# Building a product's weight operands during an earlier stage, and ordering gates and operand splits by hand, in an attention and feed-forward kernel

## Chip, cores and metric

One core of a Trainium2 chip runs the whole program in one launch. The metric is the device time of one execution in microseconds (us). PE is TensorE (matmuls), DVE VectorE, ACT ScalarE, POOL GpSimd, and SP the engine that issues all DMAs here.

## What is computed

Packed attention, then two feed-forward layers over 4608 tokens:

```python
def sm_attn(qq, kk, vv):                    # softmax(scale * q k^T) v
    ...
p_packed = sm_attn(p, k, v)                 # 8 batches x 8 heads, 32 packed rows of 64
out = sm_attn(q, p_packed, p_packed)        # 576 rows of each batch
x = out.transpose(0, 2, 1, 3).reshape(4608, 512)
x = ((x @ w_a) * (x @ w_b)) @ w_out         # 512 -> 1536 -> 512
h = x @ w_in                                # 512 -> 2048
g = h * np.clip(h + 3.0, 0.0, 6.0) / 6.0
return g @ w_out2                           # 2048 -> 512
```

All is float32; the weights reach the kernel as 64-bit words and are rounded on the chip.

## The kernel before

**Matmuls.** A float32 operand is split into `hi`, its value rounded to the matmul's type (a cast on ACT), and `lo`, the rest (a subtraction on DVE or POOL). `mm3` (L59) makes a product from three matmuls: hi by hi, hi by lo, lo by hi (L60 to L62).

**First stage: four groups of two batches.** A group has 12 steps, one for each 128 of the first layer's 1536 inner columns, 48 steps in all. A step has four `ab_unit`s (12 matmuls of 288 columns into `ab`; ACT copies one half to `a`, L440, DVE multiplies it by the other, L442, and ACT and POOL split the result `g`, L448 and L449), one `pw_unit` (32 small matmuls into `pw`, L411) and about five `y_unit`s (nine matmuls into `y`; ACT or DVE adds them up, L467 and L469). Between these lie ten slots for background work, listed in `todo` and `parts`: group one rounds the first layer's weights, groups two and three round the 32 pieces of the second layer's `w_in` and `w_out2`, and groups one to three carry the next group's attention. The order on every engine is that of the program's text; each engine works its own list in order.

**Rounding.** `f64_load` and `f64_round` (L64 to L99) take one piece of 128 x 512 words from DRAM through two ACT, three DVE and one POOL operation. `piece_units` cuts this in five units; the rounded piece, `p2f`, is stored to DRAM.

**Group four** runs `w_prep` as its background: 16 jobs, eight for `w_out2`, then eight for `w_in`. A job loads two rounded pieces into `raw_w`, makes four sums on POOL (L519 to L523), splits the seven blocks of a Strassen-like product into one tile `w` (four casts on ACT, L534, and four subtractions on DVE, L535) and stores it to `wo2d` or `w2d` in DRAM. The tile `w` has a single buffer. The last units of `bg` load y, the first layer's output, and split it for the second stage.

**Second stage.** Six blocks of 768 tokens, eight products in a block. A product takes a 256-column slice of `w_in` through seven partial products of six matmuls of 384 columns, in the order 1, 6, 2, 7, 5, 4, 3. ACT copies the first (`s`, L925), DVE adds (`u`, L776, and `b`, L948, L955, L962). `gate` (L781) is a ReLU on ACT (`r`, L784) and a minimum and multiplication on DVE (L785); two POOL operations after a product's last gate make `t2` (L967 to L969). Four products are a quad, and its *out product* (with `w_out2`) is cut into 28 units of six matmuls into `o`. While a quad's products run, one unit of the quad before follows each partial product: `o_slot` first issues the splits of the units up to two ahead (`o_split`: `oh` on ACT, L805; `ol` on DVE, L806; some with a POOL subtraction), but of no unit of a quad that is not finished, then the unit's matmuls. After the last product 28 units remain. In a block's last product `swap(k)` also splits the next block's y operands (`yh`, `yl`, L585 and L586).

```python
        def o_slot(ready):
            n = n_unit[0]
            if n >= 28 * ready:
                return
            while n_unit[1] < min(n + 1 + LEAD, 28 * ready):    # LEAD = 2
                o_split(*units[n_unit[1]])
                n_unit[1] += 1
            o_unit(*units[n])
            n_unit[0] += 1
```

Of the kernel before, what the change touches and what calls it, by code (L numbers as in the profile page):

```python
# [22 lines left out]
P = 128  # L23
# [23 lines left out]
def tile_kernel(ctx: ExitStack, tc: tile.TileContext, qT, kT, vn, pT, wab, wo1, win, wo2, out):  # L47
# [16 lines left out]
    def f64_load(pool_, src, name, bufs=AHEAD):  # L64

        raw = pool_.tile([P, CP], mybir.dt.uint64, tag="f64", name=f"f64{name}", bufs=bufs)
        sp.dma_start(raw, src)
        return raw

    def f64_round(pool_, raw, dst, name, bufs=2):  # L70
# [9 lines left out]
        def a0():  # L80
            z["sq"] = pool_.tile([P, CP], F32, tag="cv_sq", name=f"cv_sq{name}", bufs=bufs)
            act.activation(z["sq"], w.bitcast(F32), AF.Square)
            act.activation(dst.bitcast(I32), low, AF.Copy, scale=2.0 ** -13)
            z["a"] = pool_.tile([P, CP], U32, tag="cv_a", name=f"cv_a{name}", bufs=bufs)
            dve.tensor_scalar(z["a"], w, 3, 0x3FFFFFFF, op0=ALU.logical_shift_left, op1=ALU.bitwise_and)
# [18 lines left out]
    p2f = dram.tile([NM2, 2, P, CP], F32, name="p2f")  # L104
# [8 lines left out]
    es_main, es_att, es_p2a = ExitStack(), ExitStack(), ExitStack()  # L113
# [226 lines left out]
    depth = [2]  # L340
    stores = []

    def piece_load():
        k = n_piece[0]
        n_piece[0] += 1
        if k < len(pieces):
# [7 lines left out]
            raw64[k] = f64_load(att, src, f"p{m}_{i}")  # L354

    def piece_units():
# [3 lines left out]
        if m >= NM1:  # L360
            o = att.tile([P, CP], F32, tag="p2f", name=f"p2f{m}_{i}", bufs=3)
            stores.append((p2f[m - NM1, i], o))
# [9 lines left out]
        def move():  # L372
            if k > 0 and k != n_first:
                sp.dma_start(*stores[k - 1])

        u = f64_round(att, raw64.pop(k), o, f"p{m}_{i}")
        last = u.pop()

        def end():
            last()  # L380
            while n_piece[0] < n_piece[1] + depth[0]:
                piece_load()
# [3 lines left out]
        return u[:2] + [move] + u[2:] + [end]  # L386

# [96 lines left out]
    def w_tile(pool_, p, tt, n=""):  # L484
        w_t[p] = pool_.tile([P, 2, 7, 2, P], F32R, tag="w", name=f"w{n}{tt}_{p}")
# [9 lines left out]
    def w_prep(pool_, jobs):  # L495
# [3 lines left out]
        def load(i):  # L499
            def fn():  # L500
                if i == 0:
                    z["r"] = pool_.tile([P, 6, CP], F32, tag="raw", name="raw_w")
                out_, p = jobs[i]
                for j in range(2):
                    sp.dma_start(z["r"][:, 4 * (i % 2) + j], p2f[2 * p + j, int(out_)])
            return fn

        def blocks(i):
            x = z["r"].rearrange("p i (k n) -> p i k n", k=2)
            b = [x[:, 4 * (i % 2) + j, k] for j in range(2) for k in range(2)]  # L510
            if jobs[i][0]:
                b[1], b[2] = b[2], b[1]
            return b + [x[:, 2 + j, k] for j in range(2) for k in range(2)]
# [12 lines left out]
        def parts(i, of, a, n):  # L526
            def fn():
                out_, p = jobs[i]
                if a == 0:
                    z["w"] = w_tile(pool_, p, 0, f"{int(out_)}_").rearrange("p h a k n -> p h (a k n)")  # L530
# [7 lines left out]
        def store(i):  # L538
            def fn():
                out_, p = jobs[i]  # L540
                w = f32(z["w"])
                if not out_:
                    sp.dma_start(w2d[p], w.rearrange("p h x -> p (h x)"))
                    return
                for h in range(2):
                    sp.dma_start(
                        wo2d[p // QP][:, :, p % QP, h].rearrange("a p n -> p a n"), w[:, h].rearrange("p (a n) -> p a n", a=7)
                    )
            return fn

        units = [load(0)]
        for i in range(len(jobs)):
            units += [load(i + 1)] if i + 1 < len(jobs) else []
            first = [parts(i, 0, 0, 1), parts(i, 2, 1, 2)] if jobs[i][0] else [parts(i, 0, 0, 2), parts(i, 3, 2, 1)]
            units += [sums(i, 0), sums(i, 1)] + first + [parts(i, 4, 3, 2), parts(i, 6, 5, 2), store(i)]
# [131 lines left out]
    for t in range(NSTEP):  # L687
        g, m = divmod(t, NM1)
        if m == 0 and g + 1 < NG:
# [3 lines left out]
            bg = u0 + u1[:1] + [lambda b=b: at_split(b, (0,))] + u1[1:2] + [lambda b=b: at_split(b, (1,))] + u1[2:]  # L693
        if m == 0 and g + 1 == NG:
            sp.dma_start(*stores[-1])
# [3 lines left out]
            bg = w_prep(p2a, [(True, p) for p in range(NW)] + [(False, p) for p in list(range(1, NW)) + [0]])  # L699
# [13 lines left out]
        if g == 0:  # L713
            n_conv = len(by_step[m])
        else:
            n_conv = 2 * NM2 * (t - NM1 + 1) // (2 * NM1) - 2 * NM2 * (t - NM1) // (2 * NM1) if g < 3 else 0
        parts = spread(list(range(5 * n_conv)), 9 if n_conv > 2 else 6 if g > 0 or n_conv == 2 else 3) + [[]] * 7
# [4 lines left out]
        for i, (u, *x) in enumerate(units):  # L722
# [17 lines left out]
            for k in range(2):  # L740
                for _ in parts[2 * i + k]:
                    if not now:
# [14 lines left out]
    with (  # L757
# [23 lines left out]
        def gate(i, j, c, u):  # L781
# [17 lines left out]
        def o_split(Q, k, pi):  # L799
# [3 lines left out]
            hi = p2b.tile([P, TH], F32R, tag="oh", name=f"oh{Q}_{k}{pi}", bufs=4)  # L803
            lo = p2b.tile([P, TH], F32R, tag="ol", name=f"ol{Q}_{k}{pi}", bufs=4)
            act.copy(hi, x)  # L805
            dve.tensor_sub(lo, x, f32(hi))  # L806
            split_t[Q, k, pi] = (hi, lo)
# [66 lines left out]
        n_unit = [0, 0]  # L874
        LEAD = 2

        def o_slot(ready):

            n = n_unit[0]
# [132 lines left out]
```

## Time and profile before

| | |
|---|---|
| three runs | 1641.07, 1645.9, 1646.06 us; median 1645.9 |
| the profiled execution | 1646.78 us, of which 1644.9 us are the span of the profile |
| PE busy | 1504.1 us (91%), 11416 matmuls |
| DVE, ACT, POOL busy | 1076.8 us (65%), 733.8 us (45%), 745.1 us (45%) |
| mean granted clock of PE | 0.965 of full speed |
| DMA | 352.94 MB, 215 GB/s on the mean |

Engines work in parallel, so a share of busy time says which engine has least slack, not where time goes. A table by stretches gives it for one stage at a time; the views of waits say which instruction stood, and which one released it; the timeline shows single instructions, with the idle time before each in brackets. Matmuls are pipelined, so the pace of PE is read from the distance of their starts, not from their durations. In rows of operations `out<-in` are the tiles' names.

### The profile page before, as it was taken

The numbers are of one execution on the slowest core, as the hardware profiler recorded it, in microseconds if no ns is written. First come the engines' busy times: TensorE is split into PE (matmuls) and PEld (weight loads), VectorE is DVE, ScalarE is ACT, GpSimd is POOL, SyncE is SP. The second block draws the span as 40 slices with busy tenths as digits, with TensorE's granted clock in tenths as the row PEclk, the third lists the DMA queues.
The fourth block names the chain that finished last, engine by engine and source line by source line (L and its number), as shares of the span: only waits on it lengthen the run. The fifth ranks groups of instructions, "written<-read, shape, count | busy, mean of one in ns | idle before, by whom it ended". The sixth has DMA issues, their size and how long they took to land.

```text
span 1644.9 us, 29528 instructions
## 1 busy us (share of the span) xinstructions
PE 1504.1 (91%) x11416; PEld 1406.2 (85%) x11416; DVE 1076.8 (65%) x1822; ACT 733.8 (45%) x1613; POOL 745.1 (45%) x703
## 2 busy tenths in 40 slices
PE   5699999999999997888799899989989989989997
PEld 3588889999998996787789799889979979979997
DVE  5787765557646673454446766767677677676667
ACT  4566545654555544544323433443443443343333
POOL 2466564544545474555613543333352363344313
PEclk8799999999999999999799999999999999999999
DMA  8665646444554348775266656747746756765654
GB/s 272 218 212 176 205 152 210 162 167 160 190 192 164 116 141 282 245 272 220 102 240 232 258 215 252 269 172 287 289 180 253 289 189 230 287 252 224 240 200 167
DMA packets 123180, 352.94 MB, mean 215 GB/s; under 512 B 10400, under 2 KB 49312, under 8 KB 111264
## 3 DMA queue, kind: packets, MB, share of 16 engines
q1 hardware_dynamic: 123040, 351.05, 60.3%
q8 instruction: 90, 1.47, 0.4%
q14 instruction: 50, 0.41, 0.1%
HBM read 284.95 MB, written 66.06 MB: 213 GB/s over the span
## 4 chain that ended last, share of the span: by engine, by line
PE 67%; DVE 14%; ACT 6%; DMA 6%; issue 3%; POOL 3%; SPq 0%; ACTq 0%; DVEq 0%; POOLq 0%
PE o L61 6%; PE y L60 6%; PE o L62 5%; PE o L60 5%; PE y L62 5%; PE y L61 5%; PE ab L60 5%; PE ab L62 5%; PE ab L61 5%; DVE ol L806 4%; PE pw L411 2%; ACT r L784 2%; DMA w2d<-w 2%; DVE b L785 2%; DMA wo2d<-w 2%
## 5 line engine op out<-in xcount | busy, mean ns | idle before, releaser
L60 PE MATMUL ab<-at_hi,pw_hi 128*128 128x288 f32 x768 | 237.8, 310 | 37.3 <-ACT a L440 33.3
L61 PE MATMUL o<-ol,wo 128*128 128x384 f32 x672 | 237.5, 353 | 26.8 <-DVE ol L806 26.7
L60 PE MATMUL o<-oh,wo 128*128 128x384 f32 x672 | 233.5, 347 | 28.5 <-ACT oh L805 28.1
L449 POOL TENSOR_TENSOR g_lo<-g,g_hi 128x288 fp32r<-128x288 f32 x192 | 167.6, 873 | 202.8 <-ACT g_hi L448 188.1
L60 PE MATMUL y<-g_hi,wo_hi 128*128 128x288 f32 x768 | 234.0, 305 | 6.2 <-DVE acc L469 4.2
L62 PE MATMUL ab<-at_hi,pw_lo 128*128 128x288 f32 x768 | 232.2, 302 | 4.0 <-DVE pw_lo L417 4.0
L61 PE MATMUL ab<-at_lo,pw_hi 128*128 128x288 f32 x768 | 231.9, 302 | 2.3 <-DVE at_lo L293 2.3
L62 PE MATMUL o<-oh,wo 128*128 128x384 f32 x672 | 231.1, 344 | 0.0
L62 PE MATMUL y<-g_hi,wo_lo 128*128 128x288 f32 x768 | 228.1, 297 | 1.0 <-POOL wo_lo L395 1.0
L61 PE MATMUL y<-g_lo,wo_hi 128*128 128x288 f32 x768 | 228.7, 298 | 0.2 <-POOL g_lo L449 0.2
L784 ACT ACTIVATE r<-b,half_b 128x384 f32<-128x384 f32 x144 | 88.9, 617 | 288.3 <-DVE b L948 138.5
L806 DVE TENSOR_TENSOR ol<-b,oh 128x384 fp32r<-128x384 f32 x240 | 201.5, 850 | 11.8 <-ACT oh L805 11.4
L967 POOL TENSOR_TENSOR b<-b,b 128x384 f32<-128x384 f32 x48 | 58.4, 1216 | 332.3 <-DVE b L785 332.3
L60 PEld LDWEIGHTS ab<-at_hi,pw_hi 128*128 128x128 f32 x768 | 149.2, 194 | 53.7 <-ACT a L440 35.7
L442 DVE TENSOR_TENSOR g<-a,ab 128x288 f32<-128x288 f32 x192 | 86.2, 449 | 134.7 <-PE ab L62 91.7
L60 PEld LDWEIGHTS y<-g_hi,wo_hi 128*128 128x128 f32 x768 | 146.4, 191 | 25.3 <-DVE acc L469 11.2
L61 PEld LDWEIGHTS o<-ol,wo 128*128 128x128 f32 x672 | 129.8, 193 | 41.3 <-DVE ol L806 40.9
L60 PEld LDWEIGHTS o<-oh,wo 128*128 128x128 f32 x672 | 129.5, 193 | 37.1 <-ACT oh L805 37.1
L785 DVE SCALAR_TENSOR_TENSOR b<-r,b 128x384 f32<-128x384 f32 x144 | 87.5, 608 | 104.4 <-ACT r L784 104.4
L62 PEld LDWEIGHTS ab<-at_hi,pw_lo 128*128 128x128 f32 x768 | 149.5, 195 | 4.6 <-DVE pw_lo L417 4.6
L61 PEld LDWEIGHTS ab<-at_lo,pw_hi 128*128 128x128 f32 x768 | 149.6, 195 | 2.5 <-DVE at_lo L293 2.5
L62 PEld LDWEIGHTS y<-g_hi,wo_lo 128*128 128x128 f32 x768 | 146.1, 190 | 1.6 <-POOL wo_lo L395 1.5
(390 smaller groups left out, 3555.9 us busy)
## 6 DMA issues: line engine op xcount, KB each, us to landing
wo<-wo2d SPq DMA_DIRECT2D x84, 1024.0 KB, 5.6
w<-w2d SPq DMA_DIRECT2D x47, 1280.0 KB, 8.5
w<-w2d SPq DMA_DIRECT2D x47, 512.0 KB, 5.9
rab<-wabf SPq DMA_DIRECT2D x36, 512.0 KB, 5.6
f64p<-in_wo SPq DMA_DIRECT2D x28, 512.0 KB, 3.7
wo2d<-w SPq DMA_DIRECT2D x16, 896.0 KB, 5.7
w2d<-w SPq DMA_DIRECT2D x8, 1792.0 KB, 6.6
f64p<-in_wab SPq DMA_DIRECT2D x24, 512.0 KB, 4.6
```

The costliest lines, as they stand in the source:

```text
L60: pe.matmul(ps, lhsT=l_hi, rhs=r_hi, start=first, stop=False, skip_group_check=skip)
L61: pe.matmul(ps, lhsT=l_hi, rhs=r_lo, start=False, stop=False, skip_group_check=skip)
L62: pe.matmul(ps, lhsT=l_lo, rhs=r_hi, start=False, stop=last, skip_group_check=skip)
L411: pe.matmul(ps[c][o, b, :], lhsT=l[r, b, q, :], rhs=w[r, q, :], start=True, stop=True)
L442: dve.tensor_mul(g32, a, ps[1])
L449: pool.tensor_sub(gl, g32, f32(gh))
L784: act.activation(r, c, AF.Relu, bias=half_b, scale=1.0 / 6.0)
L785: dve.scalar_tensor_tensor(u, in0=r, scalar=1.0, in1=c, op0=ALU.min, op1=ALU.mult)
L806: dve.tensor_sub(lo, x, f32(hi))
L967: pool.tensor_sub(u["b12"], u["b22"], u["b12"])
```

## The change

Two things are changed. First, the operands of the out product are no longer built by group four: in groups two and three a generator, `late_units`, rounds four pieces and then runs `out_units` for a pair, ten background units at each step. `out_units` makes the sums from the rounded tiles in SBUF and splits and stores each of the seven blocks by itself (`wop`, 256 KB, three buffers). The rounding's buffers get a pool of their own, `cv1`, from group two on: two for the 64-bit words instead of four, one for `cv_sq` and `cv_a` instead of two. `w_prep` keeps the eight `w_in` jobs. Second, in the second stage the DVE half of a gate is kept in `late_` and issued by `gates()` after a later partial product's addition; the POOL operations that follow a product's last gate go with it. `o_split` becomes `o_hi` (ACT) and `o_lo` (DVE), which run up to five and four units ahead, also into the next quad where the input's gate has been issued.

```diff
+    cv = [es_cv.enter_context(tc.tile_pool(name="cv0", bufs=1, side="right"))]
+    cv_bufs = [AHEAD, 2]
...
+        def part(a):                                   # in out_units(p)
+            def fn():
+                if a > 0:
+                    sp.dma_start(wo2d[p // QP, a - 1, :, p % QP], f32(z["o"]))
+                if a < 7:
+                    z["o"] = cv[0].tile([P, 2, 256], F32R, tag="wop", name=f"wop{p}_{a}", bufs=3)
+                    act.copy(z["o"][:, 0], get(a))
+                    dve.tensor_sub(z["o"][:, 1], get(a), f32(z["o"][:, 0]))
+            return fn
+        return [sums(0), sums(1)] + [part(a) for a in range(8)]
+
+    def late_units():
+        for p in range(NM2 // 2):
+            for _ in range(4):
+                yield from piece_units()
+            yield from out_units(p)
...
+        if m == 0 and g == 1:
+            es_cv.close()
+            cv[0] = es_cv.enter_context(tc.tile_pool(name="cv1", bufs=1, side="right", reuse_waits="tile"))
+            cv_bufs[:] = [2, 1]
+            depth[0], limit[0] = 2, len(pieces)
...
-            bg = w_prep(p2a, [(True, p) for p in range(NW)] + [(False, p) for p in list(range(1, NW)) + [0]])
+            bg = w_prep(p2a, list(range(1, NW)) + [0])
...
+        n_conv = 5 * len(by_step[m]) if g == 0 else 10 if g < 3 else 0
...
             act.activation(r, c, AF.Relu, bias=half_b, scale=1.0 / 6.0)
-            dve.scalar_tensor_tensor(u, in0=r, scalar=1.0, in1=c, op0=ALU.min, op1=ALU.mult)
+            def fn():
+                dve.scalar_tensor_tensor(u[n], in0=r, scalar=1.0, in1=c, op0=ALU.min, op1=ALU.mult)
+                if n == "b12":
+                    pool.tensor_sub(u[n], u["b22"], u[n])
+                    u["t2"] = p2b.tile([P, TH], F32, tag="t2", name=f"t2{p[0]}_{p[1]}", bufs=7)
+                    pool.tensor_add(u["t2"], u[n], u["b11"])
+                u["done"].add(n)
+            late_.append(fn)
...
+        LEAD = 5
+        def o_los(to=1):
+            while n_unit[1] < min(n_unit[2], n_unit[0] + to):
+                Q, k, pi = units[n_unit[1]]
+                if k == 0 and "t2" not in u_t[Q, pi]:
+                    break
+                o_lo(*units[n_unit[1]])
+                n_unit[1] += 1
+        def o_his(to):
+            while n_unit[2] < min(len(units), n_unit[0] + to):
+                Q, k, pi = units[n_unit[2]]
+                n = OUT[ORDER[k]][1]
+                if (Q, pi) not in u_t or ("b12" if n == "t2" else n) not in u_t[Q, pi]["done"]:
+                    break
+                o_hi(*units[n_unit[2]])
+                n_unit[2] += 1
+        def o_slot():
+            o_his(1)
+            o_los(1)
+            if n_unit[0] < 28 * most[0]:
+                o_unit(*units[n_unit[0]])
+                n_unit[0] += 1
+            o_his(LEAD)
...
                 c21 = slot("b21", 6)
                 dve.tensor_add(c21, s1, y)
-                gate(1, 0, c21, c21)
+                gates()
+                gate(1, 0, c21, "b21")
+                o_los(LEAD - 1)
                 swap(4)
-                o_slot(ready)
+                o_slot()
                 some(2)
...
+        gates()
+        most[0] = NQ
         while n_unit[0] < len(units):
-            o_slot(NQ)
+            o_los(LEAD - 1)
+            o_slot()
```

How this moves instructions is shown at three places. The first is ACT at the border of two quads, in the third block: product 3 ends the first quad, product 4 begins the second (`r_3_01` is the ReLU of product 3's last gate, `s_4` the first copy of product 4, `oh_00` to `oh_03` are the `hi` of the out units whose input the first quad has just made, `oh_1x` those of the units after them). Before:

```order
L784 ACTIVATE r_3_10_14362<-b_3_14360,half_b 128x384
L784 ACTIVATE r_3_01_14379<-b_3_14377,half_b 128x384
L925 COPY s_4_14401<-h_4x 128x384
L805 CAST oh_00_14403<-b_0_13826 128x384
L805 CAST oh_01_14408<-b_1_13985 128x384
L805 CAST oh_02_14413<-b_2_14140 128x384
L805 CAST oh_03_14439<-b_3_14295 128x384
L784 ACTIVATE r_4_00_14457<-h_4x,half_b 128x384
```

With the change:

```order
L860 CAST oh_00_14462<-b_0_13981 128x384
L860 CAST oh_01_14483<-b_1_14139 128x384
L824 ACTIVATE r_3_11_14495<-b_3_14493,half_b 128x384
L860 CAST oh_02_14505<-b_2_14294 128x384
L824 ACTIVATE r_3_10_14517<-b_3_14514,half_b 128x384
L860 CAST oh_03_14527<-b_3_14449 128x384
L824 ACTIVATE r_3_01_14539<-b_3_14536,half_b 128x384
L860 CAST oh_10_14552<-t_0_14119 128x384
L1004 COPY s_4_14562<-h_4x 128x384
```

The four `oh` that stood behind `s_4` now stand before it, one between two gates of product 3.

The second place is DVE at the same border (`b_3 <- r_3_10` is the DVE half of a gate, `b_3 <- u_3,h_3z` and `u_4 <- s_4,h_4y` are additions that read a partial product, `c_` is a wide sum of the out product). Before:

```order
L955 TENSOR_TENSOR b_3_14360<-s_3_14255,h_3y 128x384
L785 SCALAR_TENSOR_TENSOR b_3_14360<-r_3_10_14362,b_3_14360 128x384
L962 TENSOR_TENSOR b_3_14377<-u_3_14277,h_3z 128x384
L785 SCALAR_TENSOR_TENSOR b_3_14377<-r_3_01_14379,b_3_14377 128x384
L867 TENSOR_TENSOR c_(0, 1)_13759<-u2o_13953,o_4_14150 128x768
L806 TENSOR_TENSOR ol_00_14404<-b_0_13826,oh_00_14403 128x384
L806 TENSOR_TENSOR ol_01_14409<-b_1_13985,oh_01_14408 128x384
L806 TENSOR_TENSOR ol_02_14414<-b_2_14140,oh_02_14413 128x384
L776 TENSOR_TENSOR u_4_14437<-s_4_14401,h_4y 128x384
```

With the change:

```order
L868 TENSOR_TENSOR ol_01_14485<-b_1_14139,oh_01_14483 128x384
L1052 TENSOR_TENSOR b_3_14536<-u_3_14427,h_3z 128x384
L827 SCALAR_TENSOR_TENSOR b_3_14514<-r_3_10_14517,b_3_14514 128x384
L868 TENSOR_TENSOR ol_02_14507<-b_2_14294,oh_02_14505 128x384
L928 TENSOR_TENSOR c_(0, 1)_13920<-u2o_14100,o_4_14300 128x768
L813 TENSOR_TENSOR u_4_14586<-s_4_14562,h_4y 128x384
L827 SCALAR_TENSOR_TENSOR b_3_14536<-r_3_01_14539,b_3_14536 128x384
L868 TENSOR_TENSOR ol_03_14529<-b_3_14449,oh_03_14527 128x384
L868 TENSOR_TENSOR ol_10_14554<-t_0_14119,oh_10_14552 128x384
```

The gate of `r_3_10` now follows the addition that was behind it, and that of `r_3_01` follows product 4's first addition; three `ol` that stood in a row come one by one.

The third place is ACT in a step of group three with out pieces (`wop` are the casts of the new pieces; `a`, `g_hi` and `acc` belong to the step's own units). Nothing stood here for them before. With the change:

```order
L485 COPY a_1_6848<-ab_10_6834 128x288
L420 CAST wop_0_6862<-p2f_1_6416 128x256
L240 COPY lhs_6214<-bd_6865 128x128
L485 COPY a_2_6882<-ab_20_6868 128x288
L493 CAST g_hi_1_6852<-g_26_1_6850 128x288
L420 CAST wop_1_6891<-p2f_1_6661 128x256
L420 CAST wop_2_6895<-p2f_1_6661 128x256
L512 COPY acc_00_6908<-y_000_6898 128x288
L493 CAST g_hi_2_6886<-g_26_2_6884 128x288
L420 CAST wop_3_6913<-s_4_6854 128x256
L512 COPY acc_10_6928<-y_010_6918 128x288
L485 COPY a_3_6944<-ab_30_6930 128x288
```

`wop_3` takes the buffer of `wop_0`, and the copy `a_3` stands behind it.

## Rows read from the trace of the kernel before

**Rows 1.** The page: the chain of work that ended last, by engine.

```profile
PE 67%; DVE 14%; ACT 6%; DMA 6%; issue 3%; POOL 3%; SPq 0%; ACTq 0%; DVEq 0%; POOLq 0%
```

**Rows 2.** Stretches: groups two and three, group four, second stage, its third block.

```profile
core 0: us, PE busy (x) PEld busy (x) DVE busy (x) ACT busy (x) POOL busy (x), PEclk, DMA share, GB/s
213.00:601.00 388.00, 386.64 (x3936) 356.30 (x3935) 243.72 (x476) 202.69 (x485) 195.60 (x210) 1.00 0.48 161
613.00:835.00 222.00, 183.86 (x1492) 171.79 (x1491) 98.48 (x187) 90.00 (x216) 112.79 (x137) 0.92 0.64 220
835.00:1640.00 805.00, 745.91 (x4034) 719.76 (x4033) 566.85 (x860) 316.14 (x629) 314.55 (x239) 0.97 0.64 239
1077.76:1211.11 133.35, 123.87 (x672) 119.78 (x673) 95.21 (x145) 53.22 (x107) 54.99 (x42) 0.97 0.65 244
```

**Rows 3.** Timeline of PE, undisturbed: start, duration, engine, line, operation.

```profile
533.24 0.29 PE L60 MATMUL ab<-at_hi,pw_hi 128*128 128x288 f32 x1
...
534.84 0.30 PE L60 MATMUL y<-g_hi,wo_hi 128*128 128x288 f32 x1
...
1139.12 0.34 PE L60 MATMUL h_3z<-yh_B,w 128*128 128x384 f32 x1
...
1140.70 0.33 PE L60 MATMUL h_4x<-yh_B,w 128*128 128x384 f32 x1
```

**Rows 4.** Matmuls of group four by line (L61, L62 alike): count, busy, mean ns, idle.

```profile
L60 PE MATMUL y<-g_hi,wo_hi 128*128 128x288 f32 x213 | 66.4, 312 | 5.5 <-DVE acc L469 4.2 <-ACT acc L467 1.2
L60 PE MATMUL ab<-at_hi,pw_hi 128*128 128x288 f32 x178 | 56.9, 320 | 32.7 <-ACT a L440 31.3 <-DVE g L442 1.4
...
L411 PE MATMUL pw<-rab,lhs 64*32 64x256 f32 x320 | 11.8, 407 | 0.0
```

**Rows 5.** Waits of PE, second stage and group four: us, times, longest.

```profile
PE o L60 <- ACT oh L805: 28.1, 22, 3.4
PE o L61 <- DVE ol L806: 26.7, 40, 1.3
...
PE ab L60 <- ACT a L440: 31.3, 8, 7.5
```

**Rows 6.** Timeline at the border of two quads in the third block.

```profile
1142.34 1.75 ACT L805 CAST oh<-b 128x384 fp32r<-128x384 f32 x4
...
1142.90 0.44 PE L60 MATMUL o<-oh,wo 128*128 128x384 f32 x1 [0.98 <-ACT oh L805]
```

**Rows 7.** Timeline of ACT and of PE in group four.

```profile
633.69 0.92 ACT L534 CAST w<-raw_w 128x256 fp32r<-128x256 f32 x2 [5.45 <-DMA wo2d<-w]
...
635.81 0.40 PE L60 MATMUL ab<-at_hi,pw_hi 128*128 128x288 f32 x1 [2.48 <-ACT a L440]
```

**Rows 8.** Waits of ACT in group four: us, times, longest.

```profile
ACT w L534 <- DMA wo2d<-w: 36.3, 8, 6.5
ACT w L534 <- DMA w2d<-w: 21.9, 7, 5.5
```

**Rows 9.** Waits of DVE in the third block.

```profile
DVE b L785 <- ACT r L784: 24.2, 30, 1.9
```

**Rows 10.** Operations of DVE in the third block: busy, mean ns, idle.

```profile
L586 DVE TENSOR_TENSOR yl_T<-ty_T,yh_T 128x768 fp32r<-128x768 f32 x4 | 4.2, 1041 | 0.2 <-ACT yh_T L585 0.2
```

**Rows 11.** Line L806 in four blocks: duration in ns, least, median, most.

```profile
L806 DVE TENSOR_TENSOR ol<-b,oh x160: 544/552/2199, 942.8 to 1472.2; 128x384 fp32r<-128x384 f32 x160
```

**Rows 12.** The jobs of group four by line: duration in ns, least, median, most.

```profile
L534 ACT CAST w<-raw_w x64: 399/619/646, 607.9 to 779.6; 128x512 fp32r<-128x512 f32 x48, 128x256 fp32r<-128x256 f32 x16
L535 DVE TENSOR_TENSOR w<-raw_w,w x64: 411/684/1247, 608.3 to 781.0; 128x512 fp32r<-128x512 f32 x48, 128x256 fp32r<-128x256 f32 x16
...
L522 POOL TENSOR_TENSOR raw_w<-raw_w x16: 722/736/747, 608.6 to 772.6; 128x256 f32<-128x256 f32 x16
```

**Rows 13.** DMA issues: KB each, median us from issue to landing.

```profile
w2d<-w SPq DMA_DIRECT2D x8, 1792.0 KB, 6.6
...
p2f<-p2f SPq DMA_DIRECT2D x32, 256.0 KB, 2.8
```

More of the change, by code (lines that the diff above doesn't have):

```diff
@@ L360, in piece_units @@
         if m >= NM1:
-            o = att.tile([P, CP], F32, tag="p2f", name=f"p2f{m}_{i}", bufs=3)
-            stores.append((p2f[m - NM1, i], o))
+            o = cv[0].tile([P, CP], F32, tag=("p2f", "w2c")[i], name=f"p2f{m}_{i}", bufs=2)
+            stores.append(None if i else (p2f[m - NM1], o))
+            w2c[m - NM1] = o
         elif i == 2:
@@ L372, in move @@
         def move():
-            if k > 0 and k != n_first:
+            if k > 0 and k != n_first and stores[k - 1]:
                 sp.dma_start(*stores[k - 1])
-        u = f64_round(att, raw64.pop(k), o, f"p{m}_{i}")
+        u = f64_round(cv[0], raw64.pop(k), o, f"p{m}_{i}")
         last = u.pop()
@@ L386, in piece_units, with out_units, get, sums @@
         return u[:2] + [move] + u[2:] + [end]
+    def out_units(p):
+        z = {}
+        def get(n):
+            return z["w"][n]
+        def sums(lo):
+            def fn():
+                if not lo:
+                    a11, a21, a12, a22 = [w2c[2 * p + i][:, k * 256:(k + 1) * 256] for i in range(2) for k in range(2)]
+                    s1, s2, s3, s4 = [cv[0].tile([P, 256], F32, tag=f"s{i}", name=f"s{i}_{p}", bufs=1) for i in range(4)]
+                    z["w"] = [a11, a12, a22, s1, s2, s3, s4]
+                    pool.tensor_add(s1, a21, a22)
+                    pool.tensor_sub(s2, s1, a11)
+                    z["a21"] = a21
+                else:
+                    pool.tensor_sub(get(5), get(0), z["a21"])
+                    pool.tensor_sub(get(6), get(1), get(4))
+            return fn
[7 more added lines that the diff above has]
+                    dve.tensor_sub(z["o"][:, 1], get(a), f32(z["o"][:, 0]))
+            return fn
+        return [sums(0), sums(1)] + [part(a) for a in range(8)]
[4 more added lines that the diff above has]
+            yield from out_units(p)
     def wo_split(t, c):
@@ L493, in w_load, with w_prep @@
             sp.dma_start(w[:, :, x], d[:, :, x])
-    def w_prep(pool_, jobs):
+    def w_prep(pool_, ps):
         z = {}
@@ L509, in blocks @@
             x = z["r"].rearrange("p i (k n) -> p i k n", k=2)
[L510 to L513, printed above, removed]
+            return [x[:, 4 * (i % 2) + j, k] for j in range(2) for k in range(2)] + [x[:, 2 + j, k] for j in range(2) for k in range(2)]
         def sums(i, lo):
@@ L538, in store @@
         def store(i):
[L539 to L549, printed above, removed]
+            return lambda: sp.dma_start(w2d[ps[i]], f32(z["w"].rearrange("p h x -> p (h x)")))
         units = [load(0)]
[L552 to L555, printed above, removed]
+        for i in range(len(ps)):
+            units += [load(i + 1)] if i + 1 < len(ps) else []
+            units += [sums(i, 0), sums(i, 1), parts(i, 0, 0, 2), parts(i, 3, 2, 1), parts(i, 4, 3, 2), parts(i, 6, 5, 2), store(i)]
         return units
@@ L711, in tile_kernel @@
         ]
[L713 to L717, printed above, removed]
+        n_conv = 5 * len(by_step[m]) if g == 0 else 10 if g < 3 else 0
+        parts = spread(list(range(n_conv)), 9 if n_conv > 10 else 6 if g > 0 or n_conv == 10 else 3) + [[]] * 7
         if g > 0:
@@ L741, in tile_kernel @@
                 for _ in parts[2 * i + k]:
+                    if g > 0:
+                        next(late)()
+                        continue
                     if not now:
@@ L896, in tile_kernel @@
                 Q, pi = divmod(tt * NW + p, QP)
-                ready = Q
+                most[0] = Q
                 more = tt + 1 < NTT
@@ L948, in tile_kernel @@
                 dve.tensor_add(c22, u3, x)
-                gate(1, 1, c22, c22)
+                gates()
+                gate(1, 1, c22, "b22")
+                o_los(LEAD - 1)
                 swap(5)
-                o_slot(ready)
+                o_slot()
                 some(2)
```

97 lines of the change are left out of this document (54 added, 43 removed).

## Prediction

> **What bounds the kernel now.** The page's chain of waits runs 67% over TensorE (PE) and 14% over VectorE (DVE) [rows 1]: PE is the bound, and the question is where it does not run at its own pace. The table by stretches splits the run [rows 2]. In groups two and three (213 to 601) PE is busy 386.6 of 388.0 us: nothing can be saved there. In group four (613 to 835) it is busy 183.9 of 222.0 us at a granted clock of 0.92, in the second stage (835 to 1640) 745.9 of 805.0 us at 0.97.
>
> Busy time hides part of the loss, since matmuls overlap; their starts give PE's pace. Undisturbed, 12 matmuls of 288 columns take from 533.24 to 534.84, 0.133 us each, and nine of 384 columns from 1139.12 to 1140.70, 0.1755 us each [rows 3]. The second stage holds 4034: 708.0 us, so **97.0 us** are lost there. Group four holds 3 x (213 + 178) = 1173 of 288 columns, 156.0 us, and 11.8 us of small pw products [rows 4]; that makes 167.8 us, so **54.2 us** are lost.
>
> What PE waits for [rows 5]: in the second stage 28.1 us for `oh`, which ScalarE (ACT) writes, and 26.7 us for DVE's `ol`, the two halves of the out product's operand, in 62 waits; in group four 31.3 us for ACT's copy `a`. A wait costs more than it shows, because a busy span of 0.34 us covers two starts. After waits the granted clock falls as well: a mean of 0.97 over 805 us is 48 us at the half level (1.2 GHz), in which half the work is done, so up to 24 us. With 59.1 us idle, some 14 are left for the restarts.
>
> Why the operands are late: at the border of two quads of products PE has run out of out work, and only then do four `oh` come in a row; the first out product has stood for 0.98 us when it gets its operand [rows 6]. In group four ACT stands 5.45 us before the `w` operands, because their one tile is still being stored to `wo2d`; the copy `a` queued behind it comes late, and PE stands for 2.48 us [rows 7]. Eight such waits (36.3 us) are for `wo2d`, seven (21.9 us) for `w2d` [rows 8].
>
> **The second stage.** Three edits act together. First, splits run up to five units ahead and across the border of two quads: in the new order the next quad's `oh` stand one by one between the gates of the last product, where four stood in a row. A unit with its product's share takes 2 x 6 x 0.1755 = 2.11 us on PE, so an `oh` has about 10 us and an `ol` about 8. Those of the old quad's inputs were finished long before; only those of the newest product come as its chain of addition, ReLU, gate and two POOL operations ends. The waits on `oh` and `ol` should nearly all go. Second, the DVE half of a gate stands behind the next product's addition, so DVE no longer idles for the ReLU: 24.2 us in one block of 133.35 us [rows 9]. Third, the two POOL operations that make `t2` come later, after the held gate; their readers are most of a product away.
>
> Nothing is added to DVE's work: 95.2 us a block [rows 2], against 672 x 0.1755 = 117.9 us for PE at pace. DVE can still be late in the last product of a block, when the next y operands are split: 4.2 us of `yl` [rows 10] on top of (95.2 - 4.2) / 8 = 11.4 us, 15.6 us in a product that PE does in 14.7, and single `ol` of up to 2.2 us [rows 11]. A PSUM tile is taken up again 3.15 us (three half-steps) after the product that filled it, so a part of this reaches PE. I take 3 us for each of five changes of block (0 to 7), 1.5 for the start, 4 for the last quad, which has no products beside it, 6 for small gaps and 3 for half clock (an eighth of 24): 29.5 us left of 97.0, a gain of **67.5 us** (ends 40 and 85).
>
> The trace shows `ol` at 552 ns in the median and 2199 at most [rows 11]. The Trainium skill has a rule for that which speaks against this change (SBUF — State Buffer, Who interferes with whom): a DVE instruction with two SBUF inputs and a GpSimd instruction that reads SBUF exclude each other for their whole length. By that rule a block's 56 `ol` and the 24 gates of like size, at 0.55, and its 4.2 us of `yl`, 48 us in all, could not overlap POOL's 55.0 [rows 2]: 103 us, still under 117.9, and the sum stays.
>
> **Group four.** The eight out jobs leave it; 77 background units instead of 141 are spread over 11 steps, 7 a step where there were 13. The `wo2d` waits go altogether. For `w2d`, four units lie between a store and the next write of its tile: 4/13 of a step before, now 4/7 of 14.0 us (167.8 / 12) = 8.0 us, against DVE's 0.7 us and 6.6 us to land [rows 12, 13]. PE bears about 3 us of ACT's waiting (5.45 against 2.48). The y transform at the end is thinned out the same way, but still waits for its load. I leave 9 of the 54.2 us: a gain of **45 us** (ends 25, if only the `wo2d` part goes, and 52).
>
> **Groups two and three.** Added are 56 casts on ACT and 56 subtractions on DVE, of 256 columns, at 0.40 and 0.41 us, and 32 POOL sums at 0.74 move here [rows 12]: 22, 23 and 24 us. ACT goes from 202.7 to 225, DVE from 243.7 to 267, POOL from 195.6 to 219 of 388 us [rows 2]: all lie beside PE's 386.6. SP issues 56 stores more and 16 fewer. Three waits are new. A piece's `wop` tile has three buffers, so ACT waits for the store three pieces back: 256 KB stores land in 2.8 us [rows 13], and the cast is due about two background slots of 1.4 us (a tenth of a step) after the issue, some 0.5 us each, inside the 3 us that PE bears. With one buffer of `cv_a`, DVE can wait for a POOL addition, for the same sort of time. And loads run two ahead, not four, with eight slots (11 us) each to land. I take 3 us; ends 0, and 25 if each of the eight steps with out pieces costs PE a wait as at 635.81 and its restart.
>
> **The sum.** The profiled execution took 1646.8 us (1.9 around the span), 0.9 over the median of the three runs. 1646.8 - 67.5 - 45 + 3 = **1537.3 us**.
>
> **Rivals.**
> 1. *DVE and POOL hold the second stage (0.20).* An addition late by over 3.15 us stops PE directly, and slow `ol` may pile up in front of it. For it: POOL and DVE both run denser. Against: 95.2 of 117.9 us, and 24 us of idling gone. If half of a block's 15.4 us (133.35 - 117.9) remains, six blocks lose 46 and start, end and half clock 14: the gain is 37, the time 1646.8 - 37 - 45 + 3 = 1568.
> 2. *Group four keeps its w2d and y waits (0.12).* For it: 1.75 MB in one tile, and 8.0 us is hardly over 7.3. Then the gain there is 25, the time 1557.
> 3. *The stores of the pieces stop ACT in groups two and three: slower (0.03).* 24 waits on `wop` (three a step in eight steps), each as the worst of group four, 7.5 us of PE [rows 5]: 180 us, and 1646.8 - 112.5 + 180 = 1714. It turns the sign from 112.5 / 24 = 4.7 us a wait. Against: these stores are 256 KB and land in 2.8 us.
> 4. *Splits don't get ahead (0.05).* If the condition on finished gates or the buffers hold them back, the second stage stays: 1646.8 - 45 + 3 = 1605. Against: the order shows them early.
>
> **How the numbers follow.** The forecast has 0.60. The range holds it with the ends of its terms (85 + 52 gained would be 1510) and rivals 1 and 2 with the end of groups two and three (1568 + 17): 1515 to 1585. Left out are rivals 3 and 4 and the far tails, under 0.2 together. Measurements of this kernel tell 0.3%, 5 us, from no change. Slower by more than that is rival 3 and a stall that I did not see, 0.04; within 0.3%, where gain and new waits cancel, 0.02; faster 0.94.
>
> **What would show it.** Right: PE's waits on `oh` and `ol` fall from 54.8 to under 15 us, DVE's wait for the ReLU in a block from 24 to a few; a block takes about 121 us; ACT's waits on `wo2d` are gone and those on `w2d` small; the second stage begins near 793 and lasts about 737; groups two and three keep their time at clock 1.00. Wrong: PE waiting for DVE's sums or ACT's `s` (rival 1), ACT for `w2d` over 15 us (rival 2), for `wo2d` in groups two and three with PE idle there (rival 3).

## The result, and the profile after

The changed kernel takes 1557.64 us in the median of four runs (1555.43 to 1558.98); the kernel before took 1643.7 us in four runs on the same chip. The ratio is 0.9475 with a 95% interval of 0.9453 to 0.9498: 86 us less, where 109.5 were forecast (1646.8 to 1537.3). The time lies in the range. The profiled execution is the one of 1555.43 us; its page has this line of engines (busy us, share of the span, instructions):

```profile
PE 1467.3 (94%) x11416; PEld 1388.8 (89%) x11416; DVE 1088.4 (70%) x1846; ACT 745.8 (48%) x1637; POOL 748.6 (48%) x703
```

Where the time went is read from three stretches that are cut alike in both traces: from the first `pw` product of group two to that of group four, from there to the second stage's first `h`, and from there to the end. The kernel before, by stretches (busy us and instructions of each engine, PE's granted clock, DMA share, GB/s):

```profile
227.50:589.20 361.70, 360.34 (x3693) 331.59 (x3692) 222.48 (x437) 188.16 (x452) 175.60 (x191) 1.00 0.49 164
589.20:835.20 246.00, 207.86 (x1718) 194.52 (x1718) 114.42 (x214) 103.19 (x246) 131.34 (x154) 0.92 0.62 213
835.20:1643.00 807.80, 746.20 (x4033) 719.72 (x4032) 567.80 (x861) 316.14 (x629) 314.55 (x239) 0.97 0.64 238
```

The changed kernel, the same view, and its third block behind them:

```profile
core 0: us, PE busy (x) PEld busy (x) DVE busy (x) ACT busy (x) POOL busy (x), PEclk, DMA share, GB/s
226.40:601.70 375.30, 365.67 (x3700) 333.77 (x3703) 256.71 (x487) 206.15 (x504) 198.68 (x221) 1.00 0.56 185
601.70:798.20 196.50, 193.03 (x1718) 183.20 (x1718) 100.91 (x188) 90.11 (x217) 106.58 (x125) 1.00 0.51 180
798.20:1550.00 751.80, 721.72 (x4034) 713.55 (x4032) 559.06 (x861) 323.38 (x629) 319.28 (x239) 0.98 0.69 256
1022.80:1148.80 126.00, 120.31 (x673) 119.28 (x673) 94.30 (x145) 54.43 (x107) 55.59 (x42) 0.97 0.70 259
```

The same matmuls run in each. Groups two and three became 13.5 us longer (361.7 to 375.2 between the starts) and PE now stands for some 10 us in them; group four became 49.4 us shorter (245.9 to 196.5), its clock going from 0.92 to 1.00; the second stage 54.8 us (805.0 to 750.2 from first to last matmul), its block of 133.35 us [rows 2] now takes 126.0. The forecast said +3, -45 and -67.5.

What PE waits for in the second stage now; before, it waited 54.8 us for `oh` and `ol`, the two halves of the out product's operand [rows 5] (us, times, longest):

```profile
PE h_0x L60 <- ACT s L1004: 24.0, 5, 5.0
PE h_7y L60 <- DVE u L813: 3.1, 5, 1.0
PE o L61 <- DVE ol L868: 0.9, 2, 0.5
PE h_4y L60 <- DMA w<-w2d: 0.8, 1, 0.8
```

The waits on `oh` and `ol` are nearly gone, and PE waits for `s` instead, some 5 us at each of the five changes of block. PE stood at these five places in the kernel before too, 3.4 us for `oh` and then 0.8 to 1.1 us for `ol` each time, 21.3 of the 54.8 us. The third change before:

```profile
1211.11 0.63 PE L60 MATMUL o<-oh,wo 128*128 128x384 f32 x1 [3.36 <-ACT oh L805]
1212.63 0.69 PE L61 MATMUL o<-ol,wo 128*128 128x384 f32 x1 [0.89 <-DVE ol L806]
```

So the stop at a change of block has not become shorter (4.2 to 4.5 us before, 4.7 to 5.0 now). The waits that fell away are the others, some 33 us. The timeline of the third change in the changed kernel, by engine (POOL, ACT, DVE, PE), shows what is late now:

```profile
1141.38 1.01 POOL L870 TENSOR_TENSOR b<-b,t 128x384 f32<-128x384 f32 x1 [2.36 <-DVE ol L868]
1142.35 1.84 POOL L606 TENSOR_TENSOR ty_T<-raw_y,ty_T 128x768 f32<-128x768 f32 x1
...
1144.22 0.83 ACT L614 CAST yh_T<-ty_T 128x768 fp32r<-128x768 f32 x1 [3.21 <-POOL ty_T L606]
...
1146.60 0.61 ACT L824 ACTIVATE r<-b,half_b 128x384 f32<-128x384 f32 x1 [1.14 <-DVE b L1052]
...
1148.26 0.47 ACT L1004 COPY s<-h_0x 128x384 f32<-128x384 f32 x1
...
1138.86 0.98 DVE L615 TENSOR_TENSOR yl_T<-ty_T,yh_T 128x768 fp32r<-128x768 f32 x1 [1.00 <-ACT yh_T L614]
...
1145.09 0.96 DVE L615 TENSOR_TENSOR yl_T<-ty_T,yh_T 128x768 fp32r<-128x768 f32 x1 [3.85 <-ACT yh_T L614]
1145.96 0.55 DVE L1052 TENSOR_TENSOR b<-u,h_7z 128x384 f32<-128x384 f32 x1
...
1141.77 0.33 PE L60 MATMUL h_0y<-yh_T,w 128*128 128x384 f32 x1
...
1148.78 0.69 PE L60 MATMUL h_0x<-yh_B,w 128*128 128x384 f32 x1 [4.73 <-ACT s L1004]
```

T4, the last of the four differences of y's blocks that the next block needs, takes a POOL subtraction (L606), whose tile `ty_T` has three buffers and so waits for T1's split on DVE (done at 1139.84). It starts only at 1142.35, because in POOL's queue a subtraction for the *next quad's* out product (L870) stands ahead of it, and that one waits 2.36 us for its own `ol`. From there it is a row of engines that each wait for one operation: ACT's cast for POOL (3.21 us) and DVE's subtraction for the cast (3.85). Behind that subtraction on DVE stands the last addition of the old block's last product (L1052), for which ACT's ReLU waits (1.14). Behind the ReLU on ACT stand a cast of y, an `oh` and then the new block's copy `s`. PE has done the new block's first two partial products by then; the third adds onto the PSUM tile that `s` has to copy first, and there PE stands. The splits that run ahead, which took the waits on `oh` and `ol` away, thus made part of this one.

In groups two and three ACT now waits for the stores of the pieces (us, times, longest); in group four hardly for any:

```profile
ACT wop L420 <- DMA wo2d<-wop: 28.4, 19, 5.9
...
ACT w L574 <- DMA w2d<-w: 0.7, 1, 0.7
```

The longest of these waits, and how it reaches PE, in the timelines of ACT, DVE and PE:

```profile
378.45 0.40 ACT L420 CAST wop<-s 128x256 fp32r<-128x256 f32 x1 [5.92 <-DMA wo2d<-wop]
...
378.88 0.43 DVE L421 TENSOR_TENSOR wop<-s,wop 128x256 fp32r<-128x256 f32 x1 [5.24 <-ACT wop L420]
379.23 0.84 DVE L258 STREAM_TRANSPOSE t<-s 128x288 f32<-128x288 f32 x2
...
379.76 0.71 PE L180 MATMUL s<-q,lhs 64*32 64x288 f32 x14 [1.67 <-DVE t L258]
```

DVE stands behind ACT for the second half of the piece, the attention's transpose stands behind that on DVE, and PE waits for the transpose.

### The profile page after: what moved, and what is told of

Its sections match the earlier page's. It is cut to its first block, busy times and chain, and to the rows that moved or that the text cites. A ratio compares the mean times of both kernels' runs of the same rounds, so it can differ in the third digit from the quotient of the medians.

```text
span 1553.1 us, 29658 instructions
## 1 busy us (share of the span) xinstructions
PE 1467.3 (94%) x11416; PEld 1388.8 (89%) x11416; DVE 1088.4 (70%) x1846; ACT 745.8 (48%) x1637; POOL 748.6 (48%) x703
## 5 line engine op out<-in xcount | busy, mean ns | idle before, releaser
L60 PE MATMUL ab<-at_hi,pw_hi 128*128 128x288 f32 x768 | 233.8, 304 | 9.0 <-ACT a L485 4.7
L60 PE MATMUL y<-g_hi,wo_hi 128*128 128x288 f32 x768 | 231.9, 302 | 0.9 <-ACT wo_hi L439 0.7
L62 PE MATMUL ab<-at_hi,pw_lo 128*128 128x288 f32 x768 | 228.5, 298 | 4.0 <-DVE pw_lo L462 4.0
L61 PE MATMUL ab<-at_lo,pw_hi 128*128 128x288 f32 x768 | 228.1, 297 | 2.3 <-DVE at_lo L295 2.3
L61 PE MATMUL o<-ol,wo 128*128 128x384 f32 x672 | 229.3, 341 | 0.9 <-DVE ol L868 0.9
L62 PE MATMUL o<-oh,wo 128*128 128x384 f32 x672 | 228.4, 340 | 0.0
L62 PE MATMUL y<-g_hi,wo_lo 128*128 128x288 f32 x768 | 227.1, 296 | 1.0 <-POOL wo_lo L440 1.0
L61 PE MATMUL y<-g_lo,wo_hi 128*128 128x288 f32 x768 | 227.6, 296 | 0.5 <-POOL g_lo L494 0.5
L60 PE MATMUL o<-oh,wo 128*128 128x384 f32 x672 | 227.2, 338 | 0.0
L60 PEld LDWEIGHTS ab<-at_hi,pw_hi 128*128 128x128 f32 x768 | 145.9, 190 | 24.8 <-issue 7.6
L60 PEld LDWEIGHTS y<-g_hi,wo_hi 128*128 128x128 f32 x768 | 144.9, 189 | 18.3 <-issue 7.0
L868 DVE TENSOR_TENSOR ol<-b,oh 128x384 fp32r<-128x384 f32 x240 | 157.8, 674 | 0.0
L62 PEld LDWEIGHTS ab<-at_hi,pw_lo 128*128 128x128 f32 x768 | 145.8, 190 | 4.5 <-DVE pw_lo L462 4.5
L61 PEld LDWEIGHTS ab<-at_lo,pw_hi 128*128 128x128 f32 x768 | 146.2, 190 | 2.5 <-DVE at_lo L295 2.5
L62 PEld LDWEIGHTS y<-g_hi,wo_lo 128*128 128x128 f32 x768 | 145.0, 189 | 1.6 <-POOL wo_lo L440 1.5
L61 PEld LDWEIGHTS y<-g_lo,wo_hi 128*128 128x128 f32 x768 | 144.9, 189 | 0.7 <-POOL g_lo L494 0.7
L485 ACT COPY a<-ab 128x288 f32<-128x288 f32 x192 | 76.5, 398 | 129.4 <-PE ab L62 128.5
L61 PEld LDWEIGHTS o<-ol,wo 128*128 128x128 f32 x672 | 127.5, 190 | 3.4 <-DVE ol L868 3.3
```

What stands on the lines that cost most here:

```text
L60: pe.matmul(ps, lhsT=l_hi, rhs=r_hi, start=first, stop=False, skip_group_check=skip)
L61: pe.matmul(ps, lhsT=l_hi, rhs=r_lo, start=False, stop=False, skip_group_check=skip)
L62: pe.matmul(ps, lhsT=l_lo, rhs=r_hi, start=False, stop=last, skip_group_check=skip)
L485: act.copy(a, ps[0])
```

## The experiments

The theory after the result has three parts: the two parts of the change add up; in the second stage PE waits only where the y operands of the next block are late, through POOL's queue; in groups two and three it pays for the stores. The rivals: the parts of the change disturb each other; the load of DVE itself is the bound; the added casts and subtractions cost the time, not the stores.

**One part alone.** Two kernels: the first stage of the change with the second stage of before, and the reverse.

> Only the first stage is changed; the second stage is that of the kernel before. By the two traces group four got 50 us shorter and groups two and three 14 us longer, so if the stages add up: 36 us under the kernel before, about 1608 us. Rival: the second stage profits from operands stored in other pieces, or the whole gain hangs together: under 1595 or over 1625.

> Only the second stage is changed; the first stage is that of the kernel before. By the two traces the second stage went from 805 to 750 us: 55 us under the kernel before, about 1589 us, with PE's waits of some 5 us at each of five changes of block. Rival as in the run beside it: under 1575 or over 1605.

Measured: 1612.19 us (ratio to before 0.980, 0.9782 to 0.9818) and 1591.06 us (0.9678, 0.9661 to 0.9694): 32.9 and 54.0 us less than the 1645.09 measured for the kernel before beside them, 86.9 together, as much as the whole change brings. The parts add up. The second stage alone shows the wait at the change of block to the tenth, `PE h_0x L60 <- ACT s L967: 24.0, 5, 5.0`: the first stage has no share in it.

**The wait at the change of block.** Two edits bring T4's subtraction forward. One makes it with the other sums, before the last product, in a fourth buffer; the other keeps three buffers and issues it right behind T1's split, ahead of the next quad's subtraction in POOL's queue:

```diff
-        first = [add("T1", ...), add("T2", ...), add("T3", ...)]       # T4 first
+        first = [add("T1", ...), add("T2", ...), add("T3", ...), add("T4", "B21", "T2")]
...
+        def part1():                                                   # T4 behind T1
+            t1()
+            t4()
-        ... 5: part("T1"), 4: part4 ...
+        ... 5: part1, 4: part("T4") ...
```

> The changed kernel, with T4 of the next block's y computed with T1 to T3 a product earlier (a fourth buffer), so that in the last product no POOL subtraction stands between T1's split and T4's. Theory (a chain: POOL's T4 waits behind a subtraction of the next quad, ACT and DVE wait for T4, the copy s behind them comes late): the 5 us waits at five block changes go, and most of the half clock after them, 25 to 35 us less: 1523 to 1533 us. Rival (the last product simply has too much work for DVE and POOL): the wait stays at 3 us or more, 1545 to 1558 us.

> The changed kernel, with T4's POOL subtraction issued right behind T1's split, before the POOL subtraction of the next quad's split, without another buffer. Theory (the chain): T4 comes 2.4 us earlier (the 1.4 us that POOL waits for ol and the 1.0 us of its subtraction), so each of five waits falls from 4.7 to about 2.3 us, with less half clock: 12 to 18 us less, about 1543 us. Rival (too much work): unchanged, 1555 to 1560 us.

Measured: 1539.07 us (0.9352, 0.9324 to 0.938) and 1534.22 us (0.9336, 0.9317 to 0.9355), 19 and 23 us less than the change. With T4 behind T1, PE's waits are:

```profile
PE h_0x L60 <- ACT s L1005: 10.7, 5, 2.4
```

Both expectations missed in size: T4 made early was to take the whole wait and left 9.6 us of 24.0, and the mere change of place did no worse, though less was expected of it. That settles the larger part: more than half of the wait was a place in POOL's queue, not a lack of a buffer, and not the load of DVE, which does the same work in both. The second stage takes 732.2 us with T4 behind T1, 18.0 less; 13.3 of them are the waits, the rest is mostly half clock after them.

**The stores.** Six of seven stores of the pieces are left out, and the last piece is stored in seven places at the end of a job; `wo2d` so holds one block seven times.

```diff
-                if a > 0:
-                    sp.dma_start(wo2d[p // QP, a - 1, :, p % QP], f32(z["o"]))
+                if a == 7:
+                    for x in range(7):
+                        sp.dma_start(wo2d[p // QP, x, :, p % QP], f32(z["o"]))
```

> The changed kernel, but the first six blocks of an out job are not stored; the last one is stored seven times at the job's end, so that the same bytes move and no piece waits for the store of the piece three back. Leaves out the stores of six of seven blocks. Theory (groups two and three got 14 us longer through ACT's waits on wop): they lose 3 us or less against the kernel before, 10 us less in all, about 1547 us. Rival (the single buffers of the rounding, or the added work itself): groups two and three stay 10 us or more over the kernel before, 1553 to 1560 us.

Measured: 1544.41 us (0.9392, 0.9368 to 0.9415). No wait of ACT for a store of a piece is left, and groups two and three take 365.0 us, 3.3 more than before the change:

```profile
226.70:591.70 365.00, 362.19 (x3700) 331.88 (x3702) 258.21 (x487) 206.11 (x504) 200.85 (x221) 1.00 0.57 190
```

The same casts, subtractions, sums and bytes are there, so of the 13.5 us the added work takes 3.3 and the waits for the stores 10.2.

**The held gate.** Its DVE half, with the two POOL operations behind a product's last gate, is issued at once again; the splits still run ahead:

```diff
-            late_.append(fn)
+            fn()
```

> The changed kernel, with the DVE half of a gate issued at once, behind its ReLU; splits still run up to five ahead. Theory (both edits are needed, since DVE's 95 us a block plus 24 us of idling are as much as PE's 118): DVE's additions come late and PE waits for them or for s, 15 to 40 us more than the changed kernel, 1572 to 1597 us. Rival (the early splits alone do it): at most 8 us more, 1557 to 1565 us.

Measured: 1574.66 us (0.9578, 0.9556 to 0.96), 17.0 us more than the change, inside what was expected. PE's waits, and DVE's in the third block:

```profile
PE h_0x L60 <- ACT s L1004: 25.8, 5, 5.5
PE h_7y L60 <- DVE u L813: 11.5, 5, 2.3
...
DVE b L827 <- ACT r L824: 22.9, 29, 1.7
```

DVE idles again for the ReLU as before [rows 9], and its additions come late where it also splits y: the h_7y wait rises from 3.1 to 11.5 us. The second stage takes 770.9 us.

**No splits across the border of two quads.** Both loops get a third limit:

```diff
-            while n_unit[2] < min(len(units), n_unit[0] + to):
+            while n_unit[2] < min(len(units), n_unit[0] + to, 28 * most[0]):
```

> The changed kernel, with no split across the border of two quads. Theory (the borders were the larger part of the waits on oh and ol): PE waits again 1.3 and 1.4 us at six borders inside blocks and some 5 us at five changes of block, where T4's subtraction is no longer behind another; against the changed kernel 10 to 20 us more, 1567 to 1577 us. Rival (the held gates and the lead inside a quad do it): within 5 us of the changed kernel or faster.

Measured: 1594.73 us (0.970, 0.9677 to 0.9723), 37 us more than the change and above the interval expected. The waits of before are back nearly whole [rows 5]:

```profile
PE o L60 <- ACT oh L860: 29.4, 12, 4.6
PE o L61 <- DVE ol L868: 21.9, 23, 1.4
```

PE no longer waits for `s` at a change of block, but it stands there all the same. At the third change:

```profile
1151.10 1.85 POOL L606 TENSOR_TENSOR ty_T<-raw_y,ty_T 128x768 f32<-128x768 f32 x1 [1.53 <-DVE yl_T L615]
...
1159.53 0.69 PE L60 MATMUL o<-oh,wo 128*128 128x384 f32 x1 [4.56 <-ACT oh L860]
```

The first line is as the theory of POOL's queue has it: without the next quad's subtraction T4's is not held up, and starts as soon as T1's split is done. The second shows that POOL's queue is not the only cause of a stop there: on ACT the four `oh` stand behind the old block's last ReLU, the cast of B22 and `s`, as they did in the kernel before. So this run measures what crossing the border is worth in all, and does not by itself confirm the theory of the change of block; the two runs with T4 earlier do.

**A shorter lead.** Two units instead of five:

```diff
-        LEAD = 5
+        LEAD = 2
```

> The changed kernel with splits at most two units ahead instead of five (an ol one unit), still across borders. Theory (crossing the border is what counts, and two units are 4.2 us against chains of 2 to 4 us): waits on oh and ol come back only where DVE or POOL are late, at changes of block and for the newest product, 5 to 15 us more than the changed kernel, 1562 to 1572 us. Rival (the distance is what counts): 25 us more or worse, over 1582 us.

Measured: 1912.13 us (1.1638, 1.1614 to 1.1662): slower than before, 340 us above what the theory allowed, and on the rival's side, 330 us beyond its bound. The view of PE's waits has one entry that says why, and the timeline shows one case of it:

```profile
PE o L61 <- DVE ol L868: 321.0, 253, 2.5
```

```profile
1303.96 0.56 DVE L813 TENSOR_TENSOR u<-s,h_0y 128x384 f32<-128x384 f32 x1 [2.36 <-PE h_0y L62]
1304.43 0.55 DVE L827 SCALAR_TENSOR_TENSOR b<-r,b 128x384 f32<-128x384 f32 x1
1304.90 1.84 DVE L868 TENSOR_TENSOR ol<-b,oh 128x384 fp32r<-128x384 f32 x2
...
1305.51 0.44 PE L61 MATMUL o<-ol,wo 128*128 128x384 f32 x1 [1.49 <-DVE ol L868]
```

The `ol` are issued LEAD - 1 units ahead counted from the unit that is about to run. With LEAD = 2 that is this very unit, and its `ol` stands in DVE's queue behind the addition of the partial product that PE has just ended: no lead at all. PE waits 253 times. The edit also cuts the buffers of `oh` and `ol` from six to three, but in the timeline DVE goes from the addition through a gate to `ol` without idling, so the place in the queue is what counts there. In the same way LEAD = 5 is a lead of three units, not four. What a lead of one unit would cost for `ol`, no run shows.

**A better version.** T4 behind T1 with a fourth buffer for the pieces (paid for by one of two buffers of `p2f`), and then also T4's split one partial product later, in the place of B22's, which goes behind the next block's first copy `s`:

```diff
-                    z["o"] = cv[0].tile([P, 2, 256], F32R, tag="wop", ..., bufs=3)
+                    z["o"] = cv[0].tile([P, 2, 256], F32R, tag="wop", ..., bufs=4)
...
-                    if last:
-                        y_part[k]()
+                    if last and k != 4:
+                        if k == 3:
+                            y_part[4]()
+                            kept.append(y_part[3])
+                        else:
+                            y_part[k]()
...
                 act.copy(s1, x)
                 o_los(LEAD - 1)
+                while kept:
+                    kept.pop()()
```

> The changed kernel with T4's subtraction right behind T1's split, and four buffers for the pieces instead of three, for one buffer less of the stored rounded tiles. Theory (waits on wop cost PE some 12 us in groups two and three): the fourth buffer gives the store one more slot of 1.4 us, half of it goes: 5 us under the kernel with T4 alone, about 1530 us. Rival (they are not what costs): the same as with T4 alone, 1534 us and more.

> The kernel with T4 right behind T1's split and four piece buffers, and in a block's last product the split of T4 one half-step later and that of B22 behind the next product's copy s, so that neither stands in front of the last addition, its ReLU or s. Theory (what is left of the wait at a change of block is this queue on DVE and ACT): the five waits of 2.1 us on s fall under 1 us: 5 to 9 us less, 1518 to 1522 us. Rival (DVE is late by its load, whatever the order): the wait stays at 2 us, 1525 to 1528 us.

Measured: 1526.75 us (0.9284, 0.9267 to 0.9301) and 1518.34 us (0.9238, 0.9217 to 0.926), as the theories had it (3 us better in the first). The fourth buffer takes ACT's waits for the stores from 28.4 to 7.7 us and groups two and three to 365.8 us, nearly what leaving out the stores gives. In the last version the waits at the changes of block are down to 1.1 us each,

```profile
PE h_0x L60 <- ACT s L1010: 5.6, 5, 1.2
...
ACT wop L420 <- DMA wo2d<-wop: 6.7, 10, 2.6
```

and its second stage, 726.6 us, runs at full clock:

```profile
787.70:1516.00 728.30, 714.89 (x4034) 703.19 (x4032) 574.00 (x861) 320.87 (x629) 327.33 (x239) 1.00 0.71 264
```

It beats both kernels: 125 us less than before, 39 less than the change.

## Why the prediction was right, and where its terms were off

The sum was 18.1 us below the profiled execution (1537.3 against 1555.43). Its terms: the second stage fell short by 12.7, groups two and three by 10.5, and group four gave 4.4 more than asked; the rest of the run, ahead of group two and behind the last matmul, gave 0.7. So the two terms that were too small miss by 23.2 us together, and what group four gave beyond its term hides a part of that. Of the signs named, the end of the waits on `oh` and `ol`, of DVE's wait for the ReLU and of ACT's waits in group four came; a block takes 126.0 us where 121 were named, groups two and three did not keep their time, and PE's wait for `s`, named as a sign of rival 1, came at the changes of block.

**The pace and the loss were right.** 4034 matmuls at 0.1755 us are 708.0 us. In the changed kernel the starts that are not at a wait or at half clock sum to 1.8 us over that pace. So the 97.0 us were indeed waits and half clock, and none of them a limit of PE's own. The half clock was the smaller part of what the prediction allowed ("up to 24 us"): in the kernel before, 105 starts lie some 0.32 us apart, which is 15 us lost.

**Splits ahead, and the held gate: right.** The waits on `oh` and `ol` were to fall under 15 us and fell from 54.8 to 0.9, though at the changes of block another wait took the place of 21.3 us of them; DVE no longer waits for the ReLU in a block, where 24.2 us were [rows 9]. Running across the border is worth 37 us and the held gate 17 us, each measured alone against the whole. The lead of `ol`, put at some 8 us, was one unit less, 6.3 us (3 x 2.11); it was enough.

**Changes of block: the mechanism half right, the size wrong.** This is the term that failed: 3 us for each of five changes and 3 us of half clock, 18 in all. Measured are five waits of 4.8 us and 8.4 us lost at half clock, 32. The prediction let all waits on `oh` and `ol` go and did not ask which of them stand at a change of block, where PE already lost 4.2 to 4.5 us each time. It looked for the new cost in DVE's load (15.6 us of work in a product of 14.7) and so priced a small excess. In the trace DVE is idle for 3.85 us just there; the stop is a chain over POOL, ACT and DVE, started by an early subtraction that waits at the head of POOL's queue. The change part named POOL's operations for `t2`, whose readers are far away, but not the POOL subtractions that the early splits carry with them, nor what stands behind these in POOL's queue.

**Small things in the second stage.** 1.5 for the start, 4 for the last quad and 6 for small gaps were forecast, 11.5; the start and the last quad show three stops of 0.4 to 0.8 us, and all that is not a wait or half clock at a change of block sums to some 10 us (42.2 lost less 32.4), the restarts after the waits among them.

**Group four: right.** The `wo2d` waits are gone, the `w2d` waits went from 21.9 us [rows 8] to 0.7, so the 8.0 us worked out between a store and the next write were enough for stores that land in 6.7 us (6.6 before [rows 13]). Of the 9 us left in this term some half remain. Rival 2 is out.

**Groups two and three: the stores were priced by their mean.** "Some 0.5 us each" is what came, 28.4 us over 56 pieces; the step that failed is "inside the 3 us that PE bears". They don't come evenly: 19 pieces wait, four of them 2.3 to 5.9 us, and those that exceed the cover reach PE, through DVE. 10.2 us of the 13.5 are theirs, by the run without stores; the 3.3 left are what was taken for the whole. The landing time in its row is a median, 2.9 us where stores of the same size landed in 2.8 before [rows 13]; the view of the tile `wop` has its spread too (least, median, most):

```profile
wo2d<-wop SPq DMA_DIRECT2D x56, 256.0 KB, 2.9
w2d<-w SPq DMA_DIRECT2D x8, 1792.0 KB, 6.7
...
DMA to landing us min/median/max: 2.3/2.9/6.9
```

The store behind the wait of 5.92 us is the slowest of them. It was issued at 371.48, right behind six loads issued from 366.74 to 369.02, of which four were still to land, the last at 377.69; it landed at 378.35. That the loads slowed it is likely, but no run without them shows it.

**The rivals.** Rival 1 put half of a block's loss at DVE and POOL together. PE did come to stand behind them, but only in a block's last product and at the change of block; elsewhere they don't bound, and the gain was 54.8 us, not the 37 it left. By the rule of the Trainium skill weighed in the prediction (SBUF — State Buffer, Who interferes with whom) the sum was to stay, and it did. The trace agrees with the rule itself: of the 336 `ol` of the changed kernel, the 224 that begin with no POOL operation under way take 0.54 to 0.56 us each, and the 112 that begin inside one end 0.41 to 0.51 us behind its end. The longest:

```profile
1128.43 1.96 POOL L615 TENSOR_TENSOR yl_B<-raw_y,yh_B 128x768 fp32r<-128x768 f32 x1 [4.04 <-ACT yh_B L614]
...
1128.59 2.22 DVE L868 TENSOR_TENSOR ol<-b,oh 128x384 fp32r<-128x384 f32 x1
```

It has a small price: this `ol`, a `yl` and another `ol` stand in DVE's queue ahead of the `u` for which PE waits 0.97 us (h_7y) in that product, and so it is at all five such waits, 3.1 us in all. Rival 3 has the right mechanism, ACT at a `wop` store, at a small part of its price: 28.4 us of ACT's time and 10 of PE's, not 180. Rival 4 is out.

## What to carry over

When an engine's work is issued ahead, look in every in-order queue that it passes, the helper engines' too, for an urgent instruction that now stands behind one that waits; the price of a change of place there was 23 us here. Price waits on a rotating buffer by the longest landing, not by the median, and ask which engine stands behind the one that waits. Before you let a row of waits go, ask at which places they stand: an instruction that no longer waits for one operand can wait at the same place for the next. Count a lead from the instruction that needs the operand and from the place in the queue where it is issued: two "units ahead" in the list were none on the engine.

## What the hardware showed that was not expected

Each stop of about 5 us at a change of block, in the middle of PE's densest work, brings a stretch at half clock (1.2 GHz): after each of the five, 7 to 15 matmuls of 384 columns start 0.32 us apart instead of 0.1755, and 8.4 us in all are lost so. At the third change:

```profile
1149.59 0.52 PE L62 MATMUL h_0x<-yh_B,w 128*128 128x384 f32 x1
1149.91 0.52 PE L60 MATMUL h_0x<-yh_B,w 128*128 128x384 f32 x1
```

With the stops cut to 2.1 to 2.4 us (T4 behind T1) three of the five still bring it, 4.0 us in all (with T4 in a fourth buffer, stops of 1.9 us, all five do); with 1.2 us and less none does. The granted clock of the second stage goes from 0.97 before to 0.98, and 1.00 in the last version. A wait is therefore worth more than it shows: 18.4 us of waiting taken away at the five changes (24.0 to 5.6) gave 23.6 us. Many short stops hardly brought half clock: in the run with LEAD = 2, PE waits 253 times for `ol`, 1.3 us on the mean and 2.5 at most, and the second stage has a granted clock of 0.99.
